# Block sums of the spatial weight in a gated mixer: two of three late sets move from GpSimd to VectorE, through the raw tiles, in the gate's second projection

## The chip, the cores and the metric

The kernel runs on one core of one Trainium2 chip. The metric is the time of one execution in device microseconds, as the median of several runs. The engines are named as the profile names them: PE is TensorE's matmul, PEld its weight load, DVE is VectorE, ACT is ScalarE, POOL is GpSimd, and SP is SyncE, which only issues transfers here. SPq, ACTq and POOLq are DMA queues of these engines.

## The reference: what is computed

The input x has 2048 rows of 512. Two branches read its layer norm, and the result is x + s * silu(g). Branch s is a local attention: 32 heads of width 16, each position looks at itself and at 7 positions before it in steps of 2. Branch g is a gated mixer whose large part is a product over positions:

```python
xn = _layernorm(x)
s = attention(xn, wqkv) @ wo
z = _gelu(xn @ w_in)                    # 2048 x 1792
z1, z2 = z[..., :896], _layernorm(z[..., 896:])
gate = einsum("ts,sf->tf", w_sp, z2) + b_sp[:, None]   # w_sp is 2048 x 2048
g = (z1 * gate) @ w_out
return x + s * silu(g)
```

All is float32.

## The kernel before

**Order of the work.** TensorE sets the order: the qkv projection (to about 150 us of the span), the gate's first projection z1 (to 216 us), the second projection z2 (216.8 to 295.7 us), the spatial mixing (297 to 590 us), the product with w_out called b (from 590.7 us), and the product with wo called s (667.5 to 711 us). The attention between qkv and s needs no matmul. It runs on VectorE, with one fold in GpSimd, at a priority below everything else, so that it fills the time that VectorE has left from 150 to 654 us. Its large operations are L550 (pr, scores), L557 (lg, a sum over a head), L594 (pv, weighted values) and the folds L604 on GpSimd and L609, L610 and L617 on VectorE, whose result tt goes to the buffer o_d.

**Float32 by halves.** TensorE multiplies float32 as three products of a high and a low half. For a weight block, fetch (L166) brings it into a tile of the tag raw, of which there are four (RAW = 4), on SP's queue. split (L190) then has ACT round it (L191, wsp_3h) and VectorE subtract (L192, wsp_3l). A raw tile is free again when all that read it is done.

**The mixing.** The product with w_sp (L787, result g) is done by block products in the manner of Strassen, so that fewer large products need sums and differences of blocks. In this order they are m1a, m1b, m2a, m2b, m6a, m6b, m7, m4, m5 and m3. m1 and m2 read blocks of w_sp itself (names wsp_0 to wsp_15); m6 and those behind it read block sums (names ws_0 to ws_7) that lie in a buffer sums_d. Block sums are made in sets: for each of two halves a of the output and each of eight i, block_sums (L390) loads four blocks of 128x512 as two tiles sa and sb of 128x1024, makes four additions of 128x512 (added, L385, whose additions are all on line L388) and stores both tiles. The sets of the first half (a = 0) and sets 0 to 4 of the second are made earlier. Sets 5, 6 and 7 of the second half are made by late_sums, called in the steps of m1a (one call for each of three steps), which puts loads, additions and stores all on GpSimd and takes the tiles from the tag t4, of which there are eight (WIDE = 8). A dependency keeps them behind the last statistics of z2. m6b is the first that reads these sums.

**The second projection.** The loop at L751 runs i from 0 to 9. For i below 8, TensorE makes z for rows i and i + 8 (z2_half, L699 to L701), and ACT evicts it with the gelu (L702). For the rows of i - 1, VectorE makes the statistics (L711, L712) and GpSimd four small operations that end in nmz (L713 to L716). For the rows of i - 2, ACT normalises (L720) and splits, and combine (L725) makes the sums of z2 that m6, m5 and m3 need: four operations of 128x384 on VectorE (L733), stored to the buffer t_d (L739, L740) and read back as the tiles tr (L836), whose split in the steps of m2a and m2b is called T3. At i = 7 the weights wsp_0 and wsp_1 of the mixing are prepared; wsp_2 and what follows is prepared as the block products come to it.

**What decides the order.** The framework schedules by priority, program order and a simulation of the engines, then every engine executes its own list strictly in order. A change in one place can thus move rows elsewhere.

The seeds (L805) are copies of ACT that put the bias into a PSUM bank before a block product adds to it.

Of the kernel before, what the change touches and what calls it, by code (L numbers as in the profile page):

```python
# [26 lines left out]
CT = 512  # L27
NC = S // CT
JC = NT // NC
HT = NT // 2  # L30
# [27 lines left out]
def kernel(  # L58
# [13 lines left out]
    nc = tc.nc  # L72
    pins = [True]

    def pin(ins):
        return tc.keep_in_program_order(ins) if pins[0] else ins
# [22 lines left out]
    sums_d = dram.tile([2, 2, HT, P, 2, CT], F32, name="sums_d")  # L99
# [46 lines left out]
    def t2(name, n=2, tag="t2", bufs=4):  # L146
        return tmp.tile([P, n * D], F32, tag=tag, name=name, bufs=bufs)
# [18 lines left out]
    def fetch(src, n, name):  # L166
        raw = raws.tile([P, 512], F32, tag="raw", name=name + "r", bufs=RAW)
        pin(nc.sync.dma_start(raw[:, :n], src))
        return raw
# [215 lines left out]
    def added(ts, eng):  # L385
        t0, t1, l0, l1 = ts
        for out_, p_, q_ in ((l1, t1, l1), (t1, t0, t1), (t0, t0, l1), (l0, t0, l0)):
            eng.tensor_tensor(out_, p_, q_, op=ALU.add)  # L388

    def block_sums(a, i, tile_=None, eng=nc.vector, loads=nc.sync, stores=nc.scalar, behind=None):  # L390
# [6 lines left out]
        for r, t in enumerate((top, low)):  # L397
            stores.dma_start(sums_d[a, r, i], t)

    def early_tile(name):  # L400
        return t2(name).rearrange("p (i t) -> p i t", i=2)

# [62 lines left out]
    for j in range(11, NT):  # L465
        if j + 2 < NT:
            fetch_cols(j + 2)
        turned = column_tile(j)
        if j == 12:
            for i in range(HT - 3):  # L470
                pool_sums(1, i, early_tile, turned, SYNC)
        low_x(j - 1, cols[j - 1])
        if j % 2:
            pair(0, j - 5)
# [28 lines left out]
    def t4(name, n=2):  # L503
        t = wide.tile([P, 2 * CT], F32, tag="t4", name=name, bufs=WIDE)
        return t.rearrange("p (i t) -> p i t", i=2)[:, :n]
# [188 lines left out]
    def z2_half(j, h, zt):  # L694
        xh, xl = xn_at(j)
        pz = mm(f"z2_{j}_{h}")[:, : WID[h]]
        for k in range(KB):
            wh, wl = [w[:, : WID[h]] for w in w2[k, h]]
            nc.tensor.matmul(pz, xh[:, k], wh, start=k == 0, stop=False)  # L699
            nc.tensor.matmul(pz, xh[:, k], wl, start=False, stop=False)  # L700
            nc.tensor.matmul(pz, xl[:, k], wh, start=False, stop=k == KB - 1)  # L701
        nc.scalar.activation(zt[:, HALF[h]], pz, AF.Gelu_apprx_tanh, scale=late_rstd(j))  # L702

    def spatial_block(c, js):
        return prep(w_sp[c, js], CT, f"wsp_{c}_{js}")

    def z2_stats(j, zt):
        st = const.tile([P, 2, 6], F32, tag="st2", name=f"zst_{j}", bufs=3)
        mv, nm = mvz[:, j], nmz[:, j : j + 1]
        for h in range(2):  # L710
            nc.vector.bn_stats(st[:, h], zt[:, h * FQ : (h + 1) * FQ])  # L711
        nc.vector.bn_aggr(mv, st)  # L712
        nc.gpsimd.tensor_tensor(nm, mv[:, 0:1], mone, op=ALU.mult)  # L713
        nc.gpsimd.tensor_scalar(mv[:, 1:2], mv[:, 1:2], EPS, None, op0=ALU.add)
        nc.gpsimd.tensor_tensor(mv[:, 1:2], mv[:, 1:2], nhalf, op=ALU.pow)
        return nc.gpsimd.tensor_tensor(nm, nm, mv[:, 1:2], op=ALU.mult)  # L716

    def z2_normal(j, zt, n):
        zh, zl = z2_at(j)
        nc.scalar.activation(zt, zt, AF.Identity, bias=nmz[:, j : j + 1], scale=mvz[:, j, 1:2])  # L720
        split(zh[:, :n], zl[:, :n], blocks(zt, FB)[:, :n])
# [3 lines left out]
    def combine(i, zts):  # L725
        b11, b12, b21, b22 = [z[:, p_] for z in zts for p_ in (first_part, last_part)]
        for out_, p_, q_, op in (
            (b11, b11, b12, ALU.subtract),
            (b12, b12, b22, ALU.subtract),
            (b22, b22, b11, ALU.add),  # L730
            (b21, b21, b22, ALU.subtract),
        ):
            nc.vector.tensor_tensor(out_, p_, q_, op=op)  # L733
        split(*[t[:, ODD + 1 :] for t in z2_at(i)], blocks(b22, ODD))
        v = b11
        src = bass.AP(
            tensor=v.tensor, offset=v.offset, ap=[list(v.ap[0]), [FH - F3, 2], [1, F3]]
        )
        nc.scalar.dma_start(t_d[:2, i].rearrange("a p t -> p a t"), src)  # L739
        nc.scalar.dma_start(t_d[2, i], b21)  # L740
# [8 lines left out]
    biases = [[b_a[:, 0], b_a[:, 1]]]  # L749
    raw_z = {}  # L750
    for i in range(HT + 2):  # L751
        if i < HT:
            raw_z[i] = [t4(f"zt_{j}").rearrange("p i t -> p (i t)")[:, :FH] for j in (i, HT + i)]
            for h in range(2):
                for j, zt in zip((i, HT + i), raw_z[i]):
                    z2_half(j, h, zt)
                if i == HT - 1 and h == 0:
                    spatial[0, 1] = spatial_block(0, 1)
        if 0 < i <= HT:
            for j, zt in zip((i - 1, HT + i - 1), raw_z[i - 1]):  # L760
                rows_known = z2_stats(j, zt)
        if i > 1:
            for j, zt, n in zip((i - 2, HT + i - 2), raw_z[i - 2], (ODD + 1, FB)):
                z2_normal(j, zt, n)
            combine(i - 2, raw_z[i - 2])
# [34 lines left out]
    for n in range(8):  # L800
        a, f = n // 2 % 2, n // 4 * 2 + n % 2
# [55 lines left out]
    def later(fn, *args):  # L857
        return lambda: fn(*args)
# [79 lines left out]
    def late_sums(i):  # L938
        return later(pool_sums, 1, i, t4, rows_known, NOSYNC)
# [1 line left out]
    block_product(  # L941
        0, "m1a", at(0, 0), plain(0, 0, 0), odd(0),
        steps=(
            [second_bias, late_sums(5)], [late_sums(6)], [second_seeds, late_sums(7)], []
        ),
    )
    oo = t4("oo")
# [75 lines left out]
    for i, j in enumerate(rows_of):  # L1023
        c, jj = divmod(j, JC)
# [98 lines left out]
```

## Time and profile before

| | |
|---|---|
| median of 3 runs | 720.09 us (719.11 to 720.56) |
| the profiled execution's own time | 716.91 us |
| its span, from first to last instruction | 715.0 us |
| PE busy, share of the span | 695.2 us, 97% |
| DVE busy | 616.9 us, 86% |
| ACT busy | 283.8 us, 40% |
| POOL busy | 184.4 us, 26% |
| mean granted TensorE clock | 0.988 |

A row of a timeline gives the start in us from the span's beginning, the length in us, the engine, the line and the operation with its output and inputs. At the end, in brackets, stands the idle time in front of it and what ended it. A group of instructions (a row that begins with a line and an engine and has "x16") gives min/median/max in ns, the starts of the first and the last one, and the shapes. Line numbers are those of the kernel before. In the order lists of the changed kernel, lines behind 398 are higher by 8 and those behind L751 by 10: L604 is L612 there, L805 is L815.

### The profile page before, as it was taken

The page shows a single profiled execution, that of the slowest core. Times are in us where ns is not written, and L with a number is a line of the kernel's source. Part 1 is how long each engine was busy: PE and PEld are TensorE (multiplying, and loading weights), DVE is VectorE, ACT ScalarE, POOL GpSimd, SP SyncE. Part 2 cuts the span into 40 slices and gives each one's busy share as a digit, 9 for nine tenths or more (in the row PEclk, how much of TensorE's full clock was granted, in tenths as well). Part 3 has the DMA queues.
Part 4 walks back from the last instruction along what each step waited for, and adds up shares of the span by engine and source line. Part 5 has one row for each costly group of instructions (what it writes and reads, how often), then busy time and mean ns, then how long its engine had stood idle before and what let it go on. Part 6 is the DMA issues. An engine that isn't in the chain of part 4 may idle for free.

```text
span 715.0 us, 9268 instructions
## 1 busy us (share of the span) xinstructions
PE 695.2 (97%) x3084; PEld 576.9 (81%) x3084; DVE 616.9 (86%) x870; ACT 283.8 (40%) x458; POOL 184.4 (26%) x174
## 2 busy tenths in 40 slices
PE   8999999999999999997998889999999999999997
PEld 7888888888888999786886668888888877888886
DVE  6774478999999998999999997989999899984474
ACT  4343332324242566781532444451433344221630
POOL 3105496211211456447541111111011101110000
PEclk9999999999999999998998999999999999999999
DMA  8769999889999431586999977658485694553994
GB/s 286 240 192 353 327 363 325 260 297 384 377 337 395 165 123 50 172 250 218 332 343 319 320 242 256 196 197 315 126 267 185 230 329 142 185 166 96 331 326 189
DMA packets 107904, 182.37 MB, mean 255 GB/s; under 512 B 10064, under 2 KB 50256, under 8 KB 107856
## 3 DMA queue, kind: packets, MB, share of 16 engines
q1 hardware_dynamic: 64800, 122.40, 51.0%
q10 hardware_dynamic: 38448, 42.60, 17.4%
q0 software_dynamic: 4608, 16.78, 6.5%
q8 instruction: 24, 0.39, 0.2%
q14 instruction: 24, 0.20, 0.1%
HBM read 122.42 MB, written 59.32 MB: 254 GB/s over the span
## 4 chain that ended last, share of the span: by engine, by line
PE 61%; DVE 18%; DMA 10%; issue 7%; ACT 2%; SPq 1%; DVEq 0%; ACTq 0%
PE g L787 6%; PE qkv L380 5%; PE qkv L382 5%; PE qkv L381 5%; PE z L674 4%; PE z L672 4%; PE z L673 4%; PE b L1018 3%; PE b L1019 3%; PE b L1017 3%; PE z L701 3%; PE z L700 3%; PE z L699 3%; DVE lg L557 3%; PE s L1019 2%
## 5 line engine op out<-in xcount | busy, mean ns | idle before, releaser
L604 POOL TENSOR_TENSOR pv<-pv 128x1024 f32<-128x1024 f32 x29 | 71.8, 2474 | 311.0 <-DVE pv L594 311.0
L550 DVE TENSOR_TENSOR pr<-k,q 128x2048 f32<-128x2048 f32 x32 | 75.4, 2355 | 7.9 <-DMA q<-qkv_d 4.1
L594 DVE TENSOR_TENSOR pv<-v,lg 128x2048 f32<-128x2048 f32 x32 | 73.2, 2289 | 1.8 <-DMA v<-qkv_d 1.2
L557 DVE TENSOR_REDUCE lg<-pr 128x128 f32<-128x2048 f32 x32 | 73.0, 2280 | 0.1
L420 ACT ACTIVATE stage<-qkv 128x512 f32<-128x512 f32 x36 | 21.4, 596 | 49.8 <-PE qkv L382 42.4
L720 ACT ACTIVATE zt<-zt,nmz,mvz 128x896 f32<-128x896 f32 x16 | 18.1, 1133 | 21.2 <-POOL nmz L716 21.2
L609 DVE TENSOR_TENSOR pv<-pv 128x512 f32<-128x512 f32 x32 | 24.0, 751 | 2.4 <-POOL pv L604 2.3
L388 POOL TENSOR_TENSOR sb<-sa,sb 128x512 f32<-128x512 f32 x16 | 22.4, 1404 | 12.4 <-DMA sb<-in_w_sp 12.0
L701 PE MATMUL z<-w_0h,BIG 128*128 128x512 f32 x64 | 25.0, 391 | 0.0
L700 PE MATMUL z<-w_0l,BIG 128*128 128x512 f32 x64 | 25.0, 391 | 0.0
L699 PE MATMUL z<-w_0h,BIG 128*128 128x512 f32 x64 | 24.9, 389 | 0.0
L1072 DVE TENSOR_TENSOR sg<-s,sg 128x512 f32<-128x512 f32 (+1 forms) x17 | 11.2, 659 | 15.7 <-PE s L1019 15.7
L713 POOL TENSOR_TENSOR nmz<-mvz,mone 128x1 f32<-128x1 f32 x16 | 12.9, 804 | 42.8 <-DVE mvz L712 42.7
L275 DVE TENSOR_TENSOR xT<-xT,mr 128x512 f32<-128x512 f32 x20 | 13.8, 688 | 11.1 <-DMA mr<-mv_d 6.9
L1028 ACT ACTIVATE bt<-b 128x512 f32<-128x512 f32 x16 | 9.4, 596 | 32.4 <-PE b L1019 32.4
L701 PE MATMUL z<-w_1h,BIG 128*128 128x384 f32 x64 | 21.5, 336 | 0.0
L700 PE MATMUL z<-w_1l,BIG 128*128 128x384 f32 x64 | 21.4, 335 | 0.0
L699 PE MATMUL z<-w_1h,BIG 128*128 128x384 f32 x64 | 21.3, 335 | 0.0
L192 DVE TENSOR_TENSOR BIG<-zt,BIG 128x512 fp32r<-128x512 f32 (+2 forms) x24 | 19.4, 814 | 1.9 <-ACT BIG L191 1.9
L191 ACT ACTIVATE BIG<-zl 128x512 fp32r<-128x512 f32 x20 | 12.3, 626 | 21.7 <-DVE zl L852 21.7
L681 ACT ACTIVATE z1t<-z 128x512 f32<-128x512 f32 x21 | 12.3, 591 | 20.9 <-DVE lg L572 7.7
L787 PE MATMUL g<-ws_7h,BIG 128*128 128x512 f32 x52 | 20.5, 403 | 0.0
(468 smaller groups left out, 2287.4 us busy)
## 6 DMA issues: line engine op xcount, KB each, us to landing
qkv_d<-stage ACTq DMA_DIRECT2D x24, 512.0 KB
k<-qkv_d SPq DMA_DIRECT2D x16, 704.0 KB
v<-qkv_d SPq DMA_DIRECT2D x16, 704.0 KB
z_d<-z1t ACTq DMA_DIRECT2D x14, 512.0 KB
zl<-z_d SPq DMA_DIRECT2D x12, 512.0 KB
tr<-t_d SPq DMA_DIRECT2D x12, 384.0 KB
x<-in_x SPq DMA_DIRECT2D x16, 256.0 KB
sa<-in_w_sp POOLq DMA_DIRECT2D x8, 512.0 KB, 6.2
```

The costliest lines, as they stand in the source:

```text
L380: nc.tensor.matmul(pq, xh[:, k], wh, start=k == 0, stop=False)
L381: nc.tensor.matmul(pq, xh[:, k], wl, start=False, stop=False)
L382: nc.tensor.matmul(pq, xl[:, k], wh, start=False, stop=k == KB - 1)
L550: line(nc.vector.tensor_tensor(pr, taps(ks[u], j0), qb.unsqueeze(1).to_broadcast([P, W, NJ * CS]), op=ALU.mult))
L557: line(nc.vector.tensor_reduce(lgs[u][:, :, j0 * HS : (j0 + NJ) * HS], pr.rearrange("p w (i d) -> p w i d", d=DH), axis=AX.X, op=ALU.add,))
L594: line(nc.vector.tensor_tensor(pv.rearrange("p w (i d) -> p w i d", d=DH), taps(vs[u], j0).rearrange("p w (i d) -> p w i d", d=DH), lgs[u] ...
L604: eng.tensor_tensor(pv[:, 0:4], pv[:, 0:4], pv[:, 4:8], op=ALU.add)
L699: nc.tensor.matmul(pz, xh[:, k], wh, start=k == 0, stop=False)
L700: nc.tensor.matmul(pz, xh[:, k], wl, start=False, stop=False)
L701: nc.tensor.matmul(pz, xl[:, k], wh, start=False, stop=k == KB - 1)
L787: nc.tensor.matmul(pg, z[a], w[b], start=start and i == 0, stop=stop and i == 2, skip_group_check=seeded)
L1019: nc.tensor.matmul(pp[:, cols], lo, wh, start=False, stop=k == n - 1)
```

## The change

Sets 5 and 6 are no longer made by late_sums. A new function raw_sums fetches the four blocks of a set into the four raw tiles on SP's queue, has VectorE make the four additions, and stores the four results on ACT's queue. It is called in the loop of the second projection, for set 5 at i = 1 and for set 6 at i = 3. Set 7 stays with GpSimd and moves from the third step of m1a to the first.

```diff
+    def raw_sums(a, i):
+        ts = [
+            fetch(w_sp[2 * a + c, r + i], CT, f"sr_{a}_{i}_{c}_{r}") for r in (0, HT) for c in range(2)
+        ]
+        added(ts, nc.vector)
+        for n, t in enumerate(ts):
+            nc.scalar.dma_start(sums_d[a, n // 2, i, :, n % 2], t)
+
...
     for i in range(HT + 2):
+        if i in (1, 3):
+            raw_sums(1, HT - 3 + i // 2)
         if i < HT:
...
         steps=(
-            [second_bias, late_sums(5)], [late_sums(6)], [second_seeds, late_sums(7)], []
+            [second_bias, late_sums(HT - 1)], [], [second_seeds], []
         ),
```

What this moves in the lists of the engines is shown at three places.

GpSimd, from the end of the second projection's small operations on, before the change. sa_5 and sb_5 are the two tiles of set 5 and their loads stand just ahead of this piece; pv_0_1531 is a fold of the attention:

```order
L393 DMA sa_6_3374<-in_w_sp 128x2x512
L388 TENSOR_TENSOR sb_5_3329<-sa_5_3328,sb_5_3329 128x512
L393 DMA sb_6_3375<-in_w_sp 128x2x512
L388 TENSOR_TENSOR sa_5_3328<-sa_5_3328 128x512
L604 TENSOR_TENSOR pv_0_1531<-pv_0_1531 128x1024
L388 TENSOR_TENSOR sa_5_3328<-sa_5_3328,sb_5_3329 128x512
L388 TENSOR_TENSOR sb_6_3375<-sa_6_3374,sb_6_3375 128x512
L388 TENSOR_TENSOR sb_5_3329<-sa_5_3328,sb_5_3329 128x512
L398 DMA sums_d<-sa_5_3328 128x1024
L393 DMA sa_7_3428<-in_w_sp 128x2x512
L388 TENSOR_TENSOR sa_6_3374<-sa_6_3374 128x512
```

The same place after the change:

```order
L393 DMA sa_7_3360<-in_w_sp 128x2x512
L393 DMA sb_7_3361<-in_w_sp 128x2x512
L612 TENSOR_TENSOR pv_0_1531<-pv_0_1531 128x1024
L388 TENSOR_TENSOR sb_7_3361<-sa_7_3360,sb_7_3361 128x512
L388 TENSOR_TENSOR sa_7_3360<-sa_7_3360 128x512
L388 TENSOR_TENSOR sa_7_3360<-sa_7_3360,sb_7_3361 128x512
L388 TENSOR_TENSOR sb_7_3361<-sa_7_3360,sb_7_3361 128x512
L398 DMA sums_d<-sa_7_3360 128x1024
L398 DMA sums_d<-sb_7_3361 128x1024
L612 TENSOR_TENSOR pv_4_1556<-pv_4_1556 128x1024
```

Set 7 has taken the place of set 5. Its four additions stand in one run, behind the fold.

SP's list of transfers, in the second projection, before the change. wsp_1r to wsp_4r are the raw tiles of weights, k and q loads of the attention:

```order
L530 DMA k_0_1445<-qkv_d 128x1408
L531 DMA q_0_1446<-qkv_d 128x512
L168 DMA wsp_1r<-in_w_sp 128x512
L168 DMA wsp_2r<-in_w_sp 128x512
L168 DMA wsp_3r<-in_w_sp 128x512
L620 DMA o_d<-tt_4_1423 32x2x128 x3
L393 DMA sa_7_2512<-in_w_sp 128x2x512
L620 DMA o_d<-tt_4_1423 32x2x128
L393 DMA sb_7_2513<-in_w_sp 128x2x512
L168 DMA wsp_4r<-in_w_sp 128x512
```

After the change the four tiles of set 5 (sr_5_...) stand in these places, and the weights come after set 6, some 18 rows later:

```order
L538 DMA k_1_1495<-qkv_d 128x1408
L539 DMA q_1_1496<-qkv_d 128x512
L168 DMA sr_6_0_0r<-in_w_sp 128x512
L168 DMA sr_6_1_0r<-in_w_sp 128x512
L628 DMA o_d<-tt_4_1469 32x2x128 x4
L168 DMA sr_6_0_8r<-in_w_sp 128x512
L168 DMA sr_6_1_8r<-in_w_sp 128x512
L168 DMA wsp_1r<-in_w_sp 128x512
L168 DMA wsp_2r<-in_w_sp 128x512
L168 DMA wsp_3r<-in_w_sp 128x512
L168 DMA wsp_4r<-in_w_sp 128x512
L628 DMA o_d<-tt_0_1504 32x2x128 x4
```

So wsp_1r to wsp_4r are no longer loaded early in the second projection but near its end, when the raw tiles of set 6 are free.

VectorE's list, in m2a and m2b, before the change. BIG<-tr is a T3 split; pr, pv and lg are attention:

```order
L192 TENSOR_TENSOR wsp_10l<-wsp_10r,wsp_10h 128x512
L192 TENSOR_TENSOR wsp_11l<-wsp_11r,wsp_11h 128x512
L550 TENSOR_TENSOR pr_0_1596<-k_1_1591,q_1_1592 128x2048
L609 TENSOR_TENSOR pv_0_1577<-pv_0_1577 128x512
L192 TENSOR_TENSOR BIG<-tr_2_3713,BIG 128x2x3x128
L610 TENSOR_TENSOR pv_0_1577<-pv_0_1577 128x4x2x32
L192 TENSOR_TENSOR wsp_12l<-wsp_12r,wsp_12h 128x512
L617 STREAM_TRANSPOSE tt_0_1600<-pv_0_1577 128x256
L192 TENSOR_TENSOR wsp_13l<-wsp_13r,wsp_13h 128x512
```

After the change:

```order
L192 TENSOR_TENSOR wsp_8l<-wsp_8r,wsp_8h 128x512
L192 TENSOR_TENSOR BIG<-tr_0_3685,BIG 128x2x3x128
L618 TENSOR_TENSOR pv_4_1556<-pv_4_1556 128x4x2x32
L192 TENSOR_TENSOR BIG<-tr_2_3725,BIG 128x2x3x128
L625 STREAM_TRANSPOSE tt_4_1565<-pv_4_1556 128x256
L594 TENSOR_REDUCE sm_1573<-lg_1499 128x32
L192 TENSOR_TENSOR BIG<-tr_4_3765,BIG 128x2x3x128
L595 RECIPROCAL sm_1573<-sm_1573 128x32
L192 TENSOR_TENSOR BIG<-tr_6_3805,BIG 128x2x3x128
L192 TENSOR_TENSOR wsp_9l<-wsp_9r,wsp_9h 128x512
L596 TENSOR_TENSOR lg_1499<-lg_1499,sm_1573 128x256
L192 TENSOR_TENSOR wsp_10l<-wsp_10r,wsp_10h 128x512
```

All four T3 splits now stand ahead of m2b's wsp_9l; before, none did, and the operation pr_0_1596 stands 15 rows behind wsp_10l where it was 2 rows behind it.

## The prediction

> **What bounds the kernel now.** I read the page's busy table first, then the waits of TensorE, and then the timelines of the engines around them.
>
> ```profile
> PE 695.2 (97%) x3084; PEld 576.9 (81%) x3084; DVE 616.9 (86%) x870; ACT 283.8 (40%) x458; POOL 184.4 (26%) x174
> ```
>
> TensorE is busy for 695.2 of 715.0 us and its number of matmuls doesn't change, so only two things can be won: its waits, and matmuls that ran at a low clock. Its waits, by what ended them (total, times, longest):
>
> ```profile
> PE g L787 <- DVE wsp_5l L192: 3.8, 1, 3.8
> PE g L787 <- DVE wsp_14l L192: 2.9, 1, 2.9
> PE g L787 <- DVE ws_7l L192: 2.6, 1, 2.6
> PE g L787 <- DVE ws_4l L192: 1.8, 1, 1.8
> PE g L787 <- ACT g L805: 1.5, 1, 1.5
> PE g L787 <- DVE ws_2l L192: 1.2, 1, 1.2
> ```
>
> They add up to 13.8 us, and all lie between 297 and 419 us: the first mixing product (m1a, m1b), the second (m2a, m2b) and m6a. Five of the six wait for VectorE, which makes the low half of a weight. The table of stretches shows why (columns: length; busy us and count of PE, PEld, DVE, ACT, POOL; granted clock, DMA share, GB/s):
>
> ```profile
> 235.00:296.00 61.00, 60.68 (x302) 54.20 (x300) 59.08 (x97) 42.58 (x64) 32.17 (x47) 1.00 0.32 108
> 297.00:335.00 38.00, 34.06 (x147) 27.59 (x148) 37.88 (x55) 19.35 (x32) 19.94 (x27) 0.98 0.71 223
> 335.00:389.00 54.00, 51.14 (x214) 41.76 (x214) 53.05 (x62) 20.23 (x34) 23.57 (x17) 0.94 0.94 327
> 389.00:419.00 30.00, 24.37 (x93) 18.78 (x92) 29.83 (x39) 12.93 (x22) 4.78 (x2) 0.90 0.92 311
> ```
>
> VectorE is full (97 to 99%) in all four rows; TensorE has nothing to wait for in the first one, the gate's second projection, and waits in the others. Behind the three waits of over 2 us the clock is low, in matmuls that follow without a gap:
>
> ```profile
> 334.60:340.60 6.00, 5.94 (x15) 4.69 (x16) 5.55 (x10) 0.63 (x2) 2.53 (x3) 0.53 0.93 307
> 388.70:395.70 7.00, 6.99 (x18) 5.50 (x19) 6.97 (x10) 2.86 (x5) 0.00 (x0) 0.56 1.00 353
> 419.00:423.50 4.50, 4.50 (x13) 3.61 (x14) 4.50 (x5) 2.20 (x4) 0.00 (x0) 0.65 0.54 173
> ```
>
> Lost there: 6.0 x 0.47 + 7.0 x 0.44 + 4.5 x 0.35 = 7.5 us. With the waits, **21.3 us** is all that this change can win on TensorE.
>
> **What it removes.** A part of VectorE's full time isn't work. These are rows of its timeline, an ordinary one first, then those that lie beside a block-sum addition on GpSimd:
>
> ```profile
> 323.44 0.68 DVE L192 TENSOR_TENSOR wsp_4l<-wsp_4r,wsp_4h 128x512 fp32r<-128x512 f32 x1
> 324.05 1.64 DVE L733 TENSOR_TENSOR zt<-zt 128x384 f32<-128x384 f32 x1
> 326.62 7.99 DVE L192 TENSOR_TENSOR wsp_5l<-wsp_5r,wsp_5h 128x512 fp32r<-128x512 f32 x1
> 335.63 2.33 DVE L733 TENSOR_TENSOR zt<-zt,zt 128x384 f32<-128x384 f32 x1
> 339.60 0.54 DVE L733 TENSOR_TENSOR zt<-zt,zt 128x384 f32<-128x384 f32 x1
> 347.17 1.45 DVE L192 TENSOR_TENSOR wsp_12l<-wsp_12r,wsp_12h 128x512 fp32r<-128x512 f32 x1 [0.25 <-ACT wsp_12h L191]
> 348.90 1.42 DVE L192 TENSOR_TENSOR wsp_13l<-wsp_13r,wsp_13h 128x512 fp32r<-128x512 f32 x1
> 350.25 2.28 DVE L594 TENSOR_TENSOR pv<-v,lg 128x2048 f32<-128x2048 f32 x1
> 354.76 3.74 DVE L550 TENSOR_TENSOR pr<-k,q 128x2048 f32<-128x2048 f32 x1
> 358.42 1.77 DVE L192 TENSOR_TENSOR wsp_14l<-wsp_14r,wsp_14h 128x512 fp32r<-128x512 f32 x1
> 360.12 1.78 DVE L609 TENSOR_TENSOR pv<-pv 128x512 f32<-128x512 f32 x1
> 361.82 1.77 DVE L192 TENSOR_TENSOR wsp_15l<-wsp_15r,wsp_15h 128x512 fp32r<-128x512 f32 x1
> ```
>
> ```profile
> 326.75 1.30 POOL L388 TENSOR_TENSOR sa<-sa 128x512 f32<-128x512 f32 x1
> 328.00 2.40 POOL L604 TENSOR_TENSOR pv<-pv 128x1024 f32<-128x1024 f32 x1
> 330.34 1.28 POOL L388 TENSOR_TENSOR sa<-sa,sb 128x512 f32<-128x512 f32 x1
> 331.57 2.47 POOL L388 TENSOR_TENSOR sb<-sa,sb 128x512 f32<-128x512 f32 x2
> ```
>
> A subtraction of 0.68 us took 7.99 us and ended (334.61) half a us behind GpSimd's run of 326.75 to 334.04; it is the one that TensorE waited 3.8 us for. With 0.68, 0.54 and 2.28 us as the ordinary lengths of 128x512, 128x384 and 128x2048, the excess is 1.10 + 7.31 + 1.79 + 0.77 + 0.74 + 1.46 + 1.09 + 1.10 + 1.09 = 16.5 us. Set 7 stays on GpSimd: its four additions are still to come at 1.3 us, 5.2 us of excess at most, now in one run, since sets 5 and 6 no longer lie between. By the order they come behind a fold of the attention, at m1b's wsp_4 and wsp_5, where the excess was 1.10 + 7.31 = 8.4. So VectorE wins 3.2 us there and 8.0 us behind it: **11.2 us**.
>
> **What it adds.** Eight additions on VectorE. The same additions of other sets ran there before:
>
> ```profile
> L388 DVE TENSOR_TENSOR sb<-sa,sb x16: 639/680/945, 155.1 to 252.1; 128x512 f32<-128x512 f32 x16
> L720 ACT ACTIVATE zt<-zt,nmz,mvz 128x896 f32<-128x896 f32 x16 | 18.1, 1133 | 21.2 <-POOL nmz L716 21.2
> ```
>
> With 0.08 us of overlap, as between 323.44 and 324.05, each takes 0.60 us, together 4.8 us, in the stretch from 235 to 296 us, where VectorE has 1.9 us left (row above). Attention covers them: it has low priority and moves back. Counted over the order, ahead of m6a's first ws_7l stand the 8 additions and one T3 split of 0.9 us more, and fewer the attention's pr, pv and lg operations of 2.2 us each and six small ones of 2.2 us together: 4.8 + 0.9 - 8.8 = -3.1 us. If that cover were gone, the 4.8 us would come off the gain. The attention's end has room: its last transpose is at 654 us, and TensorE's s product begins at 667.5 with the groups that were ready first.
>
> ```profile
> 654.03 0.45 DVE L617 STREAM_TRANSPOSE tt<-pv 128x256 f32<-128x256 f32 x1
> 667.50 0.39 PE L1017 MATMUL s<-BIG 128*128 128x512 f32 x1
> ```
>
> The transfers of 4 MB (two sets, in and out) leave the stretch with a DMA share of 0.71 to 0.94 for one with 0.32: no loss there, and nothing counted as gain. The 8 fetches on SP's queue and 8 stores on ACT's are no busy time.
>
> **What it moves.** The raw tiles are four. They held wsp_1 to wsp_4 from 227 us on, 65 us before use; now set 5 and then set 6 pass through them, and the wsp loads stand behind set 6's stores.
>
> ```profile
> 227.38 0.43 SPq L168 DMA_DIRECT2D wsp_4r<-in_w_sp  x1
> 283.85 0.60 ACT L702 ACTIVATE zt<-z 128x512 f32<-128x512 f32 x1 [1.09 <-DMA t_d<-zt]
> 294.54 0.63 ACT L191 ACTIVATE wsp_3h<-wsp_3r 128x512 fp32r<-128x512 f32 x1
> 296.47 0.61 ACT L805 ACTIVATE g<-b_a 128x512 f32<-128x512 f32 x1
> L398 ACTq DMA_DIRECT2D sums_d<-sa x8: 338/339/712, 160.5 to 251.0; - x8
> DMA to landing us min/median/max: 3.1/5.9/10.2
> ```
>
> In ACT's new order set 6's last store stands three rows ahead of z_6's first eviction, the row at 283.85: I estimate about 282 us. A store and a load of 5.9 us each, the median landing of sa's transfers, make 294, where wsp_3h stands at 294.5 now. In the new order wsp_3h and wsp_4h come ahead of z_14's two evictions, the seed of g_1 behind one eviction more (0.6 us at most), and the eight stores take ACT's queue 0.34 us each to issue, 2.7 us. TensorE already waits 1.5 us for that seed. I estimate 2 us more on it, between 0 (ACT is busy for only 42.6 of 61 us in this stretch and makes it up) and 4.5 us (2.7 + 0.6 and two copies of 0.6).
>
> **The sum on TensorE.** Of 21.3 us stay: the first wait, now 3.5; at wsp_5l, VectorE 3.2 us earlier less 2.4 of work placed ahead of it, TensorE 2 us later, so 3.8 - 0.8 - 2.0 = 1.0, with no slow clock behind it (that followed waits of 2.6 and more, not those of 1.8 and less); at ws_6l, with 2.5 us more ahead of it, VectorE comes 11.2 - 2.5 = 8.7 us earlier where TensorE would come some 12 earlier, and with half of that difference I set 1.8. That gives 21.3 - 6.3 = 15.0. VectorE allows 11.2 + 3.1 = 14.3 at ws_7l. The lower bound: the wait at wsp_5l stays whole with its clock (3.8 + 2.8), the first grows by 4.5 to 6.0, ws_6l 1.8: 21.3 - 14.4 = 6.9. Between 6.9 and 14.3 I take **11 us**, about the middle, since an order counted at ordinary lengths leaves out VectorE's waits for data. The profiled execution took 716.9 us (span 715.0), 3.2 under the median of 720.09; 11.0 from the median gives **709.1 us**.
>
> A rule on the clock can be weighed here. The slow rows are 0.53 over 6.0 us, 0.56 over 7.0 and 0.65 over 4.5. The Trainium skill, "TensorE: Matmul & The Clock Gate", Part 1, has a warm-up budget of about 3.4 us at half clock after an idle window: three of those would cost 5.1 us in place of 7.5, the gain would be 2.4 us less and the time 711.5. The first two rows are longer than that, and I keep the rows.
>
> **Rivals.** (1) *VectorE takes the waits over.* The T3 splits, four of 0.9 us, now stand ahead of m2b's wsp_9l: with the 8 additions that is 9.5 us more work there, against 11.2 won. If VectorE stands still for one late T3 load, at the 5.9 us median, the gain falls from 11 to about 5: 715 us. For it: DMA share 0.94 in that stretch. Against: more t4 tiles are free, so these loads start earlier. (2) *It doesn't do what it says:* set 7's additions in one run with the fold repeat the long block (2.4 + 5.2 = 7.6 against 7.3 us), and the later excess is only absorbed by displaced attention: 719 to 721 us. Against: seven of the nine stretched rows lie behind 335 us. (3) *Slower, by the raw tiles:* VectorE executes in order, so an addition whose fetch is late holds everything behind it. Set 6's fetches wait for set 5's stores, wsp_1 to wsp_4 for set 6's. Each hand-over is a store and a load, 11.8 us at the median landing, 20.4 at the longest. It decides once VectorE or ACT has stood for more than 14 us, all that VectorE gains; with 17 us, between one hand-over at the median and one at the longest, 720.1 + 17 - 14.3 = 722.8 us. Against: a DMA share of 0.32 there, and 21 rows of VectorE's order between set 5's last addition and set 6's first. (4) *The additions hold up GpSimd.* The stretched rows say that VectorE's two-input operations and GpSimd's additions don't run side by side. In the second projection GpSimd makes nmz, for which ACT's row above waits 21.2 us already; if each of the eight additions holds that chain for its 0.60 us and all of it reaches TensorE, the gain is 11 - 4.8 = 6.2 us and the time 713.9. Against: TensorE has no wait in that stretch to be made longer. The Trainium skill, "SBUF — State Buffer", section "Who interferes with whom", calls it an exclusive lock that goes to whoever issues first; by that VectorE can be the holder, as this rival needs, while the rows show GpSimd as the holder.
>
> **How the numbers follow.** Forecast (gain of 6 to 15.5 us) 0.56; rival 4 0.06; rival 1 (gain of 1.5 to 6) 0.18; rival 2 0.07; rival 3 0.13. The measurement can tell about 0.2%, 1.4 us, from no change. Faster 0.56 + 0.06 + 0.18 = 0.80, same 0.07, slower 0.13. The range 704.6 to 718.6 us holds the forecast and rivals 4 and 1, 0.80; it leaves out the other two.
>
> **What would show it.** Right: no VectorE subtraction of 128x512 over 1 us behind about 345 us; no wait of TensorE for wsp_14l and ws_7l, and a clock near 1 from 389 to 423; waits that sum to some 6 to 10 us, the one for the seed near 3.5. Wrong: ACT's wsp_3h or VectorE's additions waiting for a transfer; TensorE waiting for wsp_9l to wsp_13l of m2b or T3 splits; a low clock at the start of m1a; TensorE waiting in the second projection.

## The result, and the profile after

The changed kernel takes **709.62 us** (median of 4 runs, 707.55 to 712.01), the kernel before 720.33 us (4 runs, 719.11 to 721.84). The ratio is 0.985, with an interval of 0.982 to 0.989: 10.7 us faster, where 11.0 were forecast. The profiled execution of the changed kernel is the slowest of its four (712.01 us, span 710.1), and that of before is a low one (716.91), so the two traces differ by 4.9 us only. These are TensorE's waits after the change (total, times, longest):

```profile
PE g L797 <- DVE ws_6l L192: 4.2, 1, 4.2
PE z L707 <- ACT w_1h L191: 2.7, 1, 2.7
PE g L797 <- DVE wsp_1l L192: 1.8, 1, 1.8
PE g L942 <- ACT zt L710: 1.5, 1, 1.5
PE g L797 <- ACT wsp_7h L191: 0.9, 1, 0.9
PE g L797 <- ACT ws_6h L191: 0.7, 1, 0.7
```

The wait of 2.7 us for w_1h lies at 227 us, in the second projection, ahead of the new additions, and the matmuls behind it run at a low clock. It doesn't belong to the change alone: it was 1.9 us in the trace of e1 below, where TensorE, ACT, SP and VectorE have the lists of before up to the mixing, and 0.9 to 4.7 us in ten others; the trace of e3 and that of before have none. The runs don't settle what sets it. From the start of the mixing's first matmul to the end of its last, TensorE took 296.8 us before (294.1 to 590.9) and 287.6 us after (299.0 to 586.6): 9.2 us less, but it began 4.9 us later, mostly by that wait and the low clock behind it. The traces thus show 4.9 of the 10.7 us by which the medians differ. The other five waits, 9.1 us, are all in the mixing. Those for wsp_5l, wsp_14l, ws_2l, ws_4l and ws_7l are gone.

VectorE's rows that were stretched are gone with them, but for set 7's. Here nearly all of what is left, then an ordinary row and three rows of a new kind (columns as in the prediction; x3 groups three operations):

```profile
331.21 5.40 DVE L192 TENSOR_TENSOR BIG<-zt,BIG 128x896 fp32r<-128x896 f32 x3
336.54 1.77 DVE L192 TENSOR_TENSOR wsp_5l<-wsp_5r,wsp_5h 128x512 fp32r<-128x512 f32 x1
...
383.79 0.69 DVE L192 TENSOR_TENSOR wsp_14l<-wsp_14r,wsp_14h 128x512 fp32r<-128x512 f32 x1
...
406.52 0.96 DVE L192 TENSOR_TENSOR BIG<-tr,BIG 128x768 fp32r<-128x768 f32 x1 [3.61 <-ACT BIG L191]
407.40 2.29 DVE L602 TENSOR_TENSOR pv<-v,lg 128x2048 f32<-128x2048 f32 x1
409.60 2.28 DVE L565 TENSOR_REDUCE lg<-pr 128x128 f32<-128x2048 f32 x1
...
411.84 0.89 DVE L192 TENSOR_TENSOR ws_6l<-ws_6r,ws_6h 128x512 fp32r<-128x512 f32 x1
```

VectorE now stands still for 3.61 us. Behind that come two attention operations of 2.2 us, and only then ws_6l, which TensorE has been waiting for. The cause lies two engines back, in two slow loads and in the order of ACT's list. The loads are those of the tile tr and of ws_6r, issued on SP's queue:

```profile
395.17 0.37 SPq L846 DMA_DIRECT2D tr<-t_d  x1
395.77 0.56 SPq L168 DMA_DIRECT2D ws_6r<-sums_d  x1
```

ACT had to split tr before VectorE could go on. tr had landed by 403.77 us, when the next transfer that waited for it was issued. But one place ahead of the split in ACT's list stood the store g_d<-zl (L883), and by the chain of work this store waited for the load of ws_6r, which took 9.39 us. These are three rows of that chain (start, length, what), and then the timeline's row of the split; the releaser that this row names, o_d, is not the one of the chain. In the trace the load and the store have the same semaphore; no run shows whether the store had to wait for that load.

```profile
395.77 9.39 DMA ws_6r<-sums_d
405.23 0.37 ACTq L883
405.64 0.85 ACT BIG L191
```

```profile
405.64 0.85 ACT L191 ACTIVATE BIG<-tr 128x768 fp32r<-128x768 f32 x1 [3.79 <-DMA o_d<-tt]
```

The stretches after, in the same four windows (the fourth row had VectorE at 29.8 of 30 us before):

```profile
235.00:296.00 61.00, 61.00 (x304) 54.82 (x303) 58.82 (x105) 35.52 (x53) 31.59 (x50) 1.00 0.52 183
297.00:335.00 38.00, 34.71 (x144) 28.22 (x143) 35.84 (x54) 26.77 (x44) 17.29 (x23) 0.91 0.70 220
335.00:389.00 54.00, 53.14 (x235) 43.67 (x234) 51.61 (x69) 22.55 (x38) 10.25 (x7) 1.00 0.90 308
389.00:419.00 30.00, 25.12 (x104) 20.02 (x103) 26.00 (x36) 13.02 (x22) 3.07 (x2) 0.94 0.76 249
```

The DMA share went from 0.94 to 0.90 and from 0.92 to 0.76, and in the second projection from 0.32 to 0.52. VectorE is busy for 87 to 96% of the last three rows, where it was busy for 98 to 100% before. So there are two possible causes of the gain, the additions and the transfers, and the experiments are about these.

### The profile page after: what moved, and what is told of

The parts are those of the page before. It is cut to its first block, busy times and chain, and to the rows that moved or that the text cites. A ratio compares the mean times of both kernels' runs of the same rounds, so it can differ in the third digit from the quotient of the medians.

```text
span 710.1 us, 9277 instructions
## 1 busy us (share of the span) xinstructions
PE 692.7 (98%) x3084; PEld 577.0 (81%) x3084; DVE 611.5 (86%) x878; ACT 283.6 (40%) x458; POOL 166.6 (23%) x158
## 4 chain that ended last, share of the span: by engine, by line
PE 68%; DMA 15%; DVE 9%; issue 3%; ACT 2%; POOL 1%; SPq 1%; ACTq 0%; DVEq 0%
PE g L797 30%; PE qkv L382 5%; PE qkv L381 5%; PE qkv L380 5%; PE b L1027 4%; PE b L1029 4%; PE b L1028 4%; DMA z_d<-z1t 3%; PE s L1029 2%; PE s L1027 2%; PE s L1028 2%; PE z L707 2%; PE z L709 2%; DVE lg L565 2%; PE z L708 2%
## 5 line engine op out<-in xcount | busy, mean ns | idle before, releaser
L612 POOL TENSOR_TENSOR pv<-pv 128x1024 f32<-128x1024 f32 x29 | 69.6, 2401 | 338.7 <-DVE pv L602 338.7
L728 ACT ACTIVATE zt<-zt,nmz,mvz 128x896 f32<-128x896 f32 x16 | 18.2, 1134 | 19.9 <-POOL nmz L724 19.9
L192 DVE TENSOR_TENSOR BIG<-zt,BIG 128x512 fp32r<-128x512 f32 (+2 forms) x24 | 22.8, 961 | 2.1 <-ACT BIG L191 2.1
L275 DVE TENSOR_TENSOR xT<-xT,mr 128x512 f32<-128x512 f32 x20 | 13.7, 687 | 11.5 <-DMA mr<-mv_d 6.5
L1082 DVE TENSOR_TENSOR sg<-s,sg 128x512 f32<-128x512 f32 (+1 forms) x17 | 11.2, 659 | 13.4 <-PE s L1029 13.4
L721 POOL TENSOR_TENSOR nmz<-mvz,mone 128x1 f32<-128x1 f32 x16 | 9.8, 613 | 49.7 <-DVE mvz L720 49.2
L797 PE MATMUL g<-ws_6h,BIG 128*128 128x512 f32 x52 | 20.5, 401 | 0.7 <-ACT ws_6h L191 0.7
L689 ACT ACTIVATE z1t<-z 128x512 f32<-128x512 f32 x21 | 12.3, 591 | 21.0 <-DVE lg L580 7.7
L388 POOL TENSOR_TENSOR sb<-sa,sb 128x512 f32<-128x512 f32 x12 | 17.8, 1480 | 11.3 <-DMA sb<-in_w_sp 11.0
```

Source lines behind the costliest of these rows:

```text
L612: eng.tensor_tensor(pv[:, 0:4], pv[:, 0:4], pv[:, 4:8], op=ALU.add)
L797: nc.tensor.matmul(pg, z[a], w[b], start=start and i == 0, stop=stop and i == 2, skip_group_check=seeded)
```

## The experiments

**Theories.** A: GpSimd's additions hold VectorE up; this is the prediction's. B: the transfers of sets 5 and 6 in a stretch where the DMA engines are full. C: the raw tiles, as a cost of the change. D: the order of the lists, which the framework makes anew for each kernel. Times are compared with the kernel before as run beside them (medians 719.2 to 721.4 us).

For each trace I made an account of VectorE from the end of the last z2 matmul to the end of m6a's first ws_7l: held is what its operations took beyond their ordinary length, idle is the sum of its gaps (both from 297 us), and the rest is the work of its list from the end of z2 to ws_7l. VectorE works on while TensorE is late in z2, so a late end of z2 makes the rest smaller, too. Times in us.

| kernel | median | ratio to before (interval) | z2 ends | ws_7l ends | between | held | idle | rest |
|---|---|---|---|---|---|---|---|---|
| before | 720.3 | | 294.3 | 418.9 | 124.7 | 17.0 | 0.7 | 107.0 |
| changed | 709.6 | 0.985 (0.982 to 0.989) | 299.2 | 414.2 | 115.1 | 4.7 | 7.9 | 102.5 |
| e1, additions left out | 714.6 | 0.991 (0.988 to 0.994) | 298.0 | 417.6 | 119.6 | 8.0 | 5.5 | 106.1 |
| e2, idle additions | 710.1 | 0.986 (0.983 to 0.990) | 302.6 | 416.5 | 113.9 | 11.5 | 2.2 | 100.2 |
| e3, late on VectorE | 718.7 | 0.998 (0.995 to 1.001) | 295.0 | 409.8 | 114.7 | 7.5 | 2.6 | 104.6 |
| e4, all three sets raw | 723.2 | 1.003 (1.001 to 1.005) | 299.8 | 422.4 | 122.5 | 2.1 | 6.3 | 114.1 |
| e5, idle transfers | 714.8 | 0.991 (0.989 to 0.993) | 301.1 | 420.0 | 118.9 | 5.1 | 4.6 | 109.2 |
| e6, both put back | 727.1 | 1.009 (1.007 to 1.012) | 296.3 | 426.7 | 130.4 | 14.5 | 4.5 | 111.4 |
| e9, idle copies | 718.0 | 0.997 (0.994 to 0.999) | 296.2 | 415.2 | 119.0 | 5.0 | 6.7 | 107.3 |
| e10, early on GpSimd | 714.2 | 0.990 (0.987 to 0.994) | 300.9 | 411.4 | 110.5 | 8.5 | 0.8 | 101.2 |
| e12, three sets, mixed tiles | 703.4 | 0.978 (0.975 to 0.982) | 301.4 | 402.9 | 101.5 | 1.2 | 2.3 | 98.0 |

**e1, the additions left out.** In the kernel before, the additions of sets 5 and 6 are not made:

```diff
-        added([top[:, 0], top[:, 1], low[:, 0], low[:, 1]], eng)
+        if (a, i) not in ((1, 5), (1, 6)):
+            added([top[:, 0], top[:, 1], low[:, 0], low[:, 1]], eng)
```

> The kernel before, with the eight additions of sets 5 and 6 on GpSimd left out (their transfers stay, so the sums of these two sets are wrong). Theory A, GpSimd's additions hold up VectorE: the stretched VectorE rows of sets 5 and 6 go, no VectorE addition is added, TensorE's waits for wsp_5l, wsp_14l and ws_7l shrink to under 2 us each: 8 to 14 us faster than before, 706 to 712 us. Theory B, the 4 MB of transfers in the full stretch are what costs: they are all still there, so within 2 us of before, 718 to 722 us.

It gained 6.8 us (0.991), between the two ranges. Held time fell by 9.0 us. TensorE still waited, for wsp_14l longer than the 2 us of the expectation:

```profile
PE g L788 <- DVE wsp_10l L192: 4.2, 2, 3.5
PE g L788 <- DVE wsp_14l L192: 2.7, 2, 2.5
```

So the additions are a real price in the kernel before, and they aren't the whole gain of the change.

**e2, idle additions in the changed kernel.** Eight additions that nobody needs, without transfers, on GpSimd in m1a and m1b:

```diff
+    def idle_adds():
+        xs = t4("xs")
+        for n in range(8):
+            ins = nc.gpsimd.tensor_tensor(xs[:, 0], biases[0][0], biases[0][0], op=ALU.add)
+            tc.add_manual_dep(ins.ins, rows_known.ins.name, NOSYNC, reason="idle later")
...
-            [second_bias, late_sums(HT - 1)], [], [second_seeds], []
+            [second_bias, late_sums(HT - 1), idle_adds], [], [second_seeds], []
```

> The changed kernel with eight useless additions of 128x512 on GpSimd behind the last statistics, beside set 7's, without transfers. Theory A: VectorE's two-input operations there are held for up to 8 x 1.3 = 10.4 us, TensorE waits at wsp_4l to wsp_6l of m1b for 6 to 10 us more and loses some 3 us of clock: 717 to 723 us. Theory B: no transfer is added, 709 to 711 us.

710.1 us, the time of the changed kernel: theory A alone does not explain the gain. The hold is there, as these rows of VectorE show, each ordinarily of 0.68 or 0.54 us:

```profile
338.28 1.77 DVE L192 TENSOR_TENSOR wsp_6l<-wsp_6r,wsp_6h 128x512 fp32r<-128x512 f32 x1
...
341.82 1.65 DVE L741 TENSOR_TENSOR zt<-zt,zt 128x384 f32<-128x384 f32 x1
343.39 1.69 DVE L741 TENSOR_TENSOR zt<-zt 128x384 f32<-128x384 f32 x1
345.00 1.78 DVE L192 TENSOR_TENSOR wsp_8l<-wsp_8r,wsp_8h 128x512 fp32r<-128x512 f32 x1
```

In the account, held time rises by 6.8 us and idle time falls by 5.7. TensorE waits 2.3 us for m1b's wsp_7l, and no longer 4.2 for ws_6l. The more of held time took the place of idle time, and it cost nothing that can be told. Two things bound this finding. The idle additions ran from 336 to 352 us, those of the kernel before from 324 to 363. And VectorE's list ahead of ws_7l has as much attention as in the changed kernel, which isn't so in e5, e6 and e9 below.

**e3, the additions late on VectorE.** The transfers of before, at their place; only the engine of the eight additions is changed:

```diff
-        return later(pool_sums, 1, i, t4, rows_known, NOSYNC)
+        eng = nc.gpsimd if i == HT - 1 else nc.vector
+        return later(block_sums, 1, i, t4, eng, nc.gpsimd, nc.gpsimd, (rows_known, NOSYNC))
```

> The kernel before, with loads and stores of sets 5 and 6 left where they are, on GpSimd's queue in m1a, and only their eight additions on VectorE. Theory A: 11.2 us of held time go, 4.8 us of additions come in the same full stretch: a gain of about 6 us, 712 to 717 us. Theory B: transfers as before and 4.8 us more of VectorE's work where it is full: 720 to 726 us.

718.7 us: 2.7 less than before, with an interval that holds no change, and outside both ranges. Beside e1, which has no such additions, they cost 4.1 us on VectorE, where the same additions on GpSimd cost 6.8. In this place the change of engine alone is worth little.

**e5 and e9, the transfers alone.** In e5 the changed kernel has the loads and stores of sets 5 and 6 back on GpSimd's queue, to a buffer that nobody reads, without the additions. In e9 it has copies of the same number of bytes, from memory to memory, without tiles:

```diff
-            [second_bias, late_sums(HT - 1)], [], [second_seeds], []
+            [second_bias, late_sums(5, "moves")], [late_sums(6, "moves")], [second_seeds, late_sums(7)], []
```

> The changed kernel, with loads and stores as those of sets 5 and 6 put back on GpSimd's queue in m1a (into a buffer that nobody reads), without their additions. After the first runs: leaving the additions out won 6.6 us while the transfers stayed, and eight idle additions cost the changed kernel 0.4. Theory B, the rest of the gain is the transfers' place: this costs the changed kernel 4 to 8 us, 713 to 718 us, and VectorE or ACT wait longer for raw tiles. Theory D, the rest is the new order of the lists and not the transfers: 709 to 711 us.

```diff
+    def idle_copy(i):
+        for r in (0, 1, 0, 1):
+            src = w_sp[2:4, r * HT + i].rearrange("c p t -> p c t")
+            ins = nc.gpsimd.dma_start(idle_d[1, r, i], src)
+            tc.add_manual_dep(ins.ins, rows_known.ins.name, NOSYNC, reason="copy later")
...
-            [second_bias, late_sums(HT - 1)], [], [second_seeds], []
+            [second_bias, later(idle_copy, 5)], [later(idle_copy, 6)], [second_seeds, late_sums(HT - 1)], []
```

> The changed kernel with 4 MB of copies from w_sp to a buffer that nobody reads put on GpSimd's queue at the start of m1a: the bytes of the loads and stores of two sets, but without tiles and without additions. The loads and stores of e5 cost the changed kernel 5.2 us. If it is the load on the DMA engines: 713 to 718 us again. If it is the t4 tiles that they hold, or the waiting loads in GpSimd's order: 709 to 711 us.

714.8 and 718.0 us: 5.2 and 8.4 us more than the changed kernel. Both times lie in theory B's range, and tiles that the loads hold aren't needed for it, since the copies have none. The copies read and write the memory at both ends: the trace of e9 has 4.2 MB more read and 4.2 MB more written than the changed kernel's, that of e5 2.1 and 2.1. Window 340 to 380 of the changed kernel, and of e5, where the DMA share is 0.99 (in e9 it is 0.94):

```profile
340.00:380.00 40.00, 39.14 (x173) 32.07 (x172) 37.93 (x57) 19.11 (x32) 4.80 (x2) 1.00 0.95 322
```

```profile
340.00:380.00 40.00, 40.00 (x178) 33.14 (x177) 37.32 (x48) 15.96 (x26) 14.56 (x10) 1.00 0.99 357
```

In e5 TensorE pays behind that window, with a wait of 4.0 us for wsp_12l at 388 us. In e9 its longest waits lie behind it, ahead of it and in it (at 409, 301 and 377 us):

```profile
PE g L798 <- DVE ws_2l L193: 3.4, 1, 3.4
PE g L798 <- DVE wsp_1l L193: 3.3, 1, 3.3
PE g L798 <- DVE wsp_8l L193: 3.0, 1, 3.0
```

The account shows a limit of this finding. Idle time, which theory B expected to grow, did not grow in e5 and e9; the rest did, by 6.7 and 4.8 us (in e9 z2 also ended 3.0 us earlier). Counted in the traces, VectorE has 57 of the attention's large operations (128x2048, 2.28 us each) ahead of ws_7l in the changed kernel and in e2, 58 in e9, and 60 in e5, in e6 and in the kernel before. The framework plans with the transfers, so these runs don't separate what the DMA engines' load costs by itself from what the other lists cost (theory D). A full DMA stretch alone doesn't make TensorE wait: e12 below has a share of 0.95 from 340 to 380 us, and TensorE is busy throughout.

**e6, both put back.**

```diff
-            [second_bias, late_sums(HT - 1)], [], [second_seeds], []
+            [second_bias, late_sums(5, "sums")], [late_sums(6, "sums")], [second_seeds, late_sums(7)], []
```

> The changed kernel with all of GpSimd's former work on sets 5 and 6 put back, loads, additions and stores, stored to a buffer that nobody reads; VectorE's sums in the second projection stay. If held time and transfers are each enough to hold VectorE up and hide one another (theory A with B): everything that was won is lost, and 4.8 us of VectorE additions come on top: 718 to 726 us, with held time of 15 us or more between 297 and 420. If it is the order (D): 709 to 713 us.

727.1 us, 17.5 more than the changed kernel and 1.1 above the range of A with B; held time is 14.5 us, where 15 or more were expected. The additions alone cost 0.4 us and the transfers alone 5.2; together 17.5. TensorE now waits all along, mostly for VectorE:

```profile
PE g L798 <- DVE wsp_1l L193: 3.4, 1, 3.4
PE g L798 <- DVE ws_5l L193: 2.6, 1, 2.6
PE g L798 <- DVE wsp_13l L193: 2.6, 2, 2.1
```

**e10, early on GpSimd.** The changed kernel with one word changed:

```diff
-        added(ts, nc.vector)
+        added(ts, nc.gpsimd)
```

> The changed kernel with the additions of sets 5 and 6 on GpSimd in place of VectorE, still from the raw tiles in the second projection. If the place is what counts and not the engine: 708 to 712 us. If GpSimd's additions cost VectorE there what they cost in the mixing (8 x 1.3 = 10.4 us held in place of 4.8 us of additions) and hold up nmz: 713 to 720 us.

714.2 us, in the second range, 4.6 more than on VectorE and 6.7 less than before (0.990): place and engine both count; which counts more is within the noise.

**e7, e4, e8, e11 and e12, the tiles.** e7 moves set 5 only:

```diff
-        if i in (1, 3):
+        if i == 1:
...
-            [second_bias, late_sums(HT - 1)], [], [second_seeds], []
+            [second_bias], [late_sums(6)], [second_seeds, late_sums(7)], []
```

> Half of the change: only set 5 goes through the raw tiles to VectorE, at i = 1; sets 6 and 7 stay with GpSimd in the second and third step of m1a. A with B: about half of the gain, 713 to 717 us. Raw tiles (C): wsp_1r to wsp_4r wait for one set in place of two, so TensorE's waits at the start of m1a, 3.3 us in the changed kernel, fall below 2 us.

717.6 us: 3.2 of the 10.7 us, just outside the range. At the start of m1a TensorE waited 2.1 and 1.3 us, as long as with two sets, so this wait isn't in proportion to the sets that pass through the raw tiles; that expectation failed, too. e4 moves all three:

```diff
-        if i in (1, 3):
+        if i in (1, 3, 5):
...
-            [second_bias, late_sums(HT - 1)], [], [second_seeds], []
+            [second_bias], [], [second_seeds], []
```

> The changed kernel with set 7 moved too, by raw_sums at i = 5, so that GpSimd adds nothing in the mixing. Theory A alone: the last 5.2 us of held time in m1b go, 2.4 us of VectorE additions come in the second projection: 704 to 709 us. Rival C, the raw tiles: wsp_1r to wsp_4r are loaded one store and one load (11.8 us) later, TensorE waits 5 to 12 us at the start of m1a and loses 3 us of clock: 712 to 722 us.

723.2 us, slower than before: the prediction's rival 3, in m1a. wsp_3r is issued at 318 where the changed kernel issued it at 287 us, and ACT, which executes in order, comes to it at 326:

```profile
318.19 0.38 SPq L168 DMA_DIRECT2D wsp_3r<-in_w_sp  x1
```

```profile
326.55 0.61 ACT L191 ACTIVATE wsp_3h<-wsp_3r 128x512 fp32r<-128x512 f32 x1
```

```profile
PE g L942 <- ACT zt L710: 6.9, 2, 4.3
PE g L797 <- ACT wsp_3h L191: 5.4, 1, 5.4
...
PE g L797 <- DVE wsp_3l L192: 3.2, 1, 3.2
```

e8 takes the two sets out of the raw tiles and puts them into t4 tiles:

```diff
-            raw_sums(1, HT - 3 + i // 2)
+            block_sums(1, HT - 3 + i // 2, t4)
```

> The changed kernel with sets 5 and 6 on VectorE in the same place of the program, but in two tiles of the tag t4 each in place of the four raw tiles, so that wsp_1r to wsp_4r are loaded early as before. C: the waits of 3.3 us at the start of m1a and some 2 us of low clock behind them go: 703 to 708 us. Against it: z2 and these sums share eight t4 tiles; if that holds up the evictions of z2, TensorE waits in the second projection and the time is 711 to 718 us.

713.1 us (0.988, interval 0.983 to 0.993), not to be told from the changed kernel. The mixing took 279.6 us in place of 287.6, but TensorE waited in the second projection for ACT's evictions (5.0 us in two waits). Since VectorE went on working during these waits, the two numbers are not independent. e11 has set 5 in raw tiles and set 6 in t4 tiles:

```diff
-            raw_sums(1, HT - 3 + i // 2)
+            (raw_sums if i == 1 else block_sums)(1, HT - 3 + i // 2, *([t4] if i == 3 else []))
```

> The changed kernel with set 5 through the raw tiles at i = 1 as it is and set 6 in two t4 tiles at i = 3, as in e8. There the mixing took 279.6 us in place of 287.6, but the second projection was held up by waits of 4.4 and 0.6 us for t4 tiles. If one set leaves enough t4 tiles: no wait of over 1 us in the second projection behind 230 us, 704 to 709 us. If it doesn't: 710 to 715 us.

712.2 us (0.988, interval 0.983 to 0.993), in the upper range, though the wait for evictions fell to 0.8 us; instead TensorE waited 2.2 us in m6 and 4.0 for w_1h. e12 adds set 7 to this, through the raw tiles, so that no transfer and no addition of these sets is left in the mixing:

```diff
-        if i in (1, 3):
-            raw_sums(1, HT - 3 + i // 2)
+        if i in (1, 3, 5):
+            (block_sums if i == 3 else raw_sums)(1, HT - 3 + i // 2, *([t4] if i == 3 else []))
...
-            [second_bias, late_sums(HT - 1)], [], [second_seeds], []
+            [second_bias], [], [second_seeds], []
```

> All three sets on VectorE in the second projection: sets 5 and 7 through the raw tiles, set 6 in two t4 tiles, so that wsp_1r to wsp_4r wait for one set less than in e4. After e5 and e9, another 2 MB of transfers out of the mixing should be worth 2 to 4 us against e11 and the changed kernel: 704 to 709 us, with TensorE's waits in m1a and m1b below 5 us. If the raw tiles or VectorE's 12 additions make TensorE wait in m1a as in e4 (over 10 us): 714 to 722 us.

**703.4 us** (6 runs, 702.36 to 705.12; ratio 0.978, interval 0.975 to 0.982): faster than both kernels, and 0.6 us below the lower range; 2 to 4 us were expected against e11 and the changed kernel, and it is 8.8 and 6.2. The run takes set 7's additions off GpSimd as well, so it doesn't show how much of this is the transfers'. The mixing takes 275.5 us. Of these waits the first two lie in the second projection, the last two in the mixing:

```profile
PE z L707 <- ACT zt L710: 3.0, 1, 3.0
PE z L707 <- ACT w_1h L191: 1.5, 1, 1.5
...
PE g L942 <- ACT zt L710: 1.0, 1, 1.0
PE g L797 <- DVE wsp_5l L192: 0.5, 1, 0.5
```

```profile
340.00:380.00 40.00, 40.00 (x178) 33.15 (x177) 38.56 (x55) 19.12 (x31) 4.82 (x2) 1.00 0.95 328
380.00:420.00 40.00, 40.00 (x178) 33.11 (x178) 39.27 (x51) 19.12 (x32) 7.22 (x3) 1.00 0.78 270
```

TensorE is busy through both windows at the full clock. The 296.8 us of before less the 13.8 us of waits and the 7.5 us of clock, the 21.3 us that the prediction called all that can be won, are 275.5. That it agrees to the tenth is chance, since 1.5 us of waits are left. And a part is paid for elsewhere: the second projection, with its waits of 3.0 and 1.5 us, ends 7.1 us later than before, so that the span is 14.1 us shorter (700.9 for 715.0).

## Why the prediction came out, point by point

The time was right. That it came within 0.3 us is luck: 11 was taken as about the middle between 6.9 and 14.3, the sum was right in its first term, and others were off, most of them to the costly side.

- *VectorE's held time.* 16.5 us before and 5.2 left were forecast; 17.0 and 4.7 were counted. The gain of 11.2 was 12.3 us. The stretched rows behind 345 us are gone, as the test in the prediction asked.
- *The waits that go.* wsp_14l, ws_7l, ws_4l and ws_2l are gone. The clock near 1 that the test asked for from 389 to 423 us did not come: it is 0.94 in the row from 389 to 419 (0.90 before), with a low stretch behind the new wait for ws_6l. The wait for wsp_5l was to shrink to 1.0 us; it is gone too.
- *The start of m1a.* The wait was forecast at 3.5 us, for the seed, and is 1.82 + 1.47 = 3.3; but the wait for the seed is gone, and these are two others, so the number came by luck. No late load of a raw tile shows in them. ACT made wsp_1h at 297.24 us without having stood idle for a load, and VectorE came to wsp_1l only behind two attention operations (the second stands below) and sums of z2. The eviction that the second wait is for stands behind wsp_3h and wsp_4h, as the prediction had read from the order, and behind a table load of 1.28 us; a step of the attention (L588), with a table load of its own at 295.62, has come between the evictions. One set gave the same two waits (e7). What was missed is the clock behind them, 5.5 x 0.50 = 2.8 us, set out below; the prediction had named it as a sign of being wrong.

```profile
297.24 0.62 ACT L191 ACTIVATE wsp_1h<-wsp_1r 128x512 fp32r<-128x512 f32 x1
297.94 2.28 DVE L565 TENSOR_REDUCE lg<-pr 128x128 f32<-128x2048 f32 x1
301.40 0.68 DVE L192 TENSOR_TENSOR wsp_1l<-wsp_1r,wsp_1h 128x512 fp32r<-128x512 f32 x1
302.24 1.28 ACT L710 ACT_TABLE_LOAD   x1
303.53 0.98 ACT L710 ACTIVATE zt<-z 128x512 f32<-128x512 f32 x2
```

- *ws_6l.* 1.8 us was forecast and 4.2 came, and not from work placed ahead of it alone: VectorE stood still first, behind ACT, for the slow loads of tr and ws_6r. Rival 1 had that mechanism (a late load in front of VectorE) at the T3 splits; it came later, in m6a, and the time stayed within the forecast.
- *VectorE's allowance.* 14.3 us (11.2 held, 3.1 by order) was forecast at ws_7l. It became 12.3 of held time and 4.5 of order, less 7.2 of new idle time: 9.6. The cut from 14.3 to 11 "since an order counted at ordinary lengths leaves out VectorE's waits for data" was the right kind of cut, though a little small for this trace. The 4.5 us hold a part that isn't order, since z2 ended 4.9 us later after the change and VectorE worked on meanwhile.
- **The weakest step** is "no loss there, and nothing counted as gain", on the 4 MB of transfers. Put back alone they cost 5.2 and 8.4 us (e5, e9), the additions alone 0.4 (e2), both 17.5 (e6). The prediction read the row with a DMA share of 0.94 and TensorE's waits in it, and put these waits down to the engine named last. Five waits named VectorE, and VectorE was full. It may have been full in part because the lists are planned around transfers: e5 has 60 large attention operations ahead of ws_7l, as before, where the changed kernel has 57. These three fewer stood already in the prediction's 3.1 us by order, so it is open how much of the transfers' price its sum left out.
- *Rival 2* (nothing changes) gave the additions of set 7 the power to repeat the long block. They did hold VectorE (5.40 us for three operations of 2.05 us together), between m1b's wsp_4l and wsp_5l, and TensorE didn't wait there.
- *Rival 3* was the right mechanism for a kernel that goes one set further (e4), in m1a and at 2 us over before.
- *Rival 4* left no trace: in the second projection VectorE's operations were held 1.9 us after, 3.0 before (beyond the median length of their kind), and ACT's waits for nmz went from 21.2 to 19.9 us.
- *What is shown and what is open.* Put back into the changed kernel, the additions cost nothing that can be told, the transfers, with the lists that come with them, a half to four fifths of the gain, and both together more than all of it (the 4.8 us of VectorE's additions stay in e6 and buy nothing there). In the kernel before, the additions alone were worth 6.8 us (e1). Open is how much of the transfers' price is load on the DMA engines and how much the lists that are planned with them.

## What to carry to other kernels

When a full engine's waits disappear, ask what it will wait for next before adding up the gain: here 12.3 us of held time gave 7.2 back as idle time. A step that is moved out of a crowded stretch takes its transfers along, and these, with the order that is planned around them, can be worth more than its arithmetic; price them by a run that has the transfers alone, one that has the arithmetic alone, and one that has both, since the three don't add up. Where a buffer's tiles are shared with the next stage, don't send everything through it: with one of three sets in other tiles (e12) the same move took 703.4 us, with all three in the raw tiles (e4) 723.2.

## What the runs showed of the hardware

**The length of a wait alone doesn't tell whether the clock goes low.** The prediction took from the waits of before that up to 1.8 us leave the clock alone, and 2.6 and more don't. After the change, 1.82 and 1.47 us, 2.4 us apart, were followed by eleven matmuls of 0.63 us in place of 0.39:

```profile
302.13 0.50 PE L797 MATMUL g<-wsp_1l,BIG 128*128 128x512 f32 x1 [1.82 <-DVE wsp_1l L192]
...
302.71 0.39 PE L797 MATMUL g<-wsp_2h,BIG 128*128 128x512 f32 x1
304.56 0.79 PE L942 MATMUL g<-BIG 128*128 128x512 f32 x1 [1.47 <-ACT zt L710]
305.15 0.63 PE L797 MATMUL g<-wsp_2l,BIG 128*128 128x512 f32 x1
...
309.42 0.63 PE L797 MATMUL g<-wsp_1h,BIG 128*128 128x512 f32 x1
...
310.17 0.39 PE L797 MATMUL g<-wsp_1h,BIG 128*128 128x512 f32 x1
```

```profile
304.50:310.00 5.50, 5.44 (x13) 4.28 (x14) 5.50 (x7) 5.50 (x12) 0.00 (x0) 0.50 0.70 211
```

The granted clock is 0.50 over the whole of 303.2 to 310.0 us, 6.8 us, and TensorE stood still in it until 304.56; behind the wait of 4.2 us for ws_6l it is 0.50 from 412.5 to 415.8. In e1 a single wait of 1.94 us, for w_1h, was followed by a clock of 0.51 (226 to 229 us), and one of 2.54 us, for wsp_14l, by a clock of 1.00 (367.8 to 371 us). What decides is not shown.

Half the clock for 5.5 us is longer than the 3.4 us that the Trainium skill ("TensorE: Matmul & The Clock Gate", Part 1) gives as a warm-up budget; this is the third such row of the case.

**VectorE and GpSimd take turns in these rows.** Beside a run of GpSimd additions, each of VectorE's two-input operations takes about 1.7 us in place of 0.6 (e2's rows above): its own time and one addition of 1.3 us, less an overlap. The case of before, 7.99 us for one subtraction, was a wait through five GpSimd operations in a row, four additions and a fold (the prediction's rows). "SBUF — State Buffer" of the Trainium skill ("Who interferes with whom") has it as a lock held for one instruction; the rows of e2 agree with that, and the 7.99 us row shows that the waiting engine can lose several rounds.
